# Sixteen extra short loads of K, issued once from SyncE in a single-core attention kernel

## The chip, the cores and the metric

The kernel runs on one core of a Trainium2 chip. The metric is the device time of one execution in microseconds (us), the median of several. A core has a matrix engine (TensorE, PE in the profile), VectorE (DVE), ScalarE (ACT), GpSimd (POOL) and SyncE (SP), each with its own instruction stream, and 16 DMA engines that move data between HBM and the on-chip memory. SyncE and ScalarE issue DMAs here; what SyncE issues goes to queue q1 of the profile, what ScalarE issues goes to q10.

## The reference

```python
B, H, Sq, Skv, Dh = 8, 16, 16, 2048, 256
def reference(q, k, v):
    scale = q.shape[-1] ** -0.5
    scores = jnp.einsum('bhqd,bhkd->bhqk', q, k) * scale
    attn = _softmax(scores, axis=-1)
    return jnp.einsum('bhqk,bhkd->bhqd', attn, v)
```

All tensors are bf16. K and V are 134 MB each, q and the output 1 MB each. Every element of K and V is used once, with only 16 queries per head.

## The kernel before

The 128 heads are worked off in 16 blocks of 8 heads (the loop index is g, r or j, `last` is 15). A block needs 16,384 rows of K and as many of V. The rows lie contiguously in HBM, so a load gives each of the 128 partitions one contiguous piece: K of a block comes in two DMAs of 4 MB (half blocks e = 0 and 1, 32 KB a partition, `load_k`, line 127), V of a block in one DMA of 8 MB (64 KB a partition, `load_v`, line 133). The last two blocks' V is cut into 3 and 9 pieces.

The on-chip tile SL has four slots of 4 MB: two hold V (VA, VB), two hold K (KA, KB). There is one buffer for each, so a load can only be issued when the matmuls that read the previous contents have ended. For a block, VectorE transposes K in place (line 196), PE forms Q·K (lines 309 and 310), VectorE takes the maximum, ScalarE the exponential, VectorE transposes the result, ScalarE and VectorE copy it into weights, and PE multiplies by V (line 332, 128 matmuls); ScalarE scales the result and stores it with a DMA on its own queue (line 301).

PE works Q·K of block r, then P·V of block r - 1. SyncE's stream follows this: after the first loads it runs a loop over j from 2 to 14 (line 143). A pass waits on c_qk (Q·K of half e of block j - 1 is done) and issues K of block j, for e = 0 and 1, then waits on c_pv (P·V of block j - 2 is done) and issues V of block j - 1. Nothing else stands in SyncE's stream there. After the loop come the last block's K in four pieces, the pieces of V for the last two blocks, and then a wait on c_ev (ScalarE has scaled the last result, line 155), the last store (line 156) and the wait for its landing (line 157).

A load tells that it is done through a semaphore: 16 are added for each DMA. The completion semaphores of K and V are s_k and s_v and their relatives; VectorE waits for K, PE for V.

Of the kernel before, what the change touches and what calls it, by code (L numbers as in the profile page):

```python
# [11 lines left out]
BF16 = mybir.dt.bfloat16  # L12
# [8 lines left out]
def bass_standalone__softmax_full_bidir__sampling_kernel(  # L21
# [16 lines left out]
    ku = k.rearrange("b h s d -> (b h s) d").rearrange("(u p t) d -> u p t d", p=128, t=T)  # L38
# [4 lines left out]
    with ExitStack() as es:  # L43
        ec = es.enter_context
# [9 lines left out]
        PTz = ec(nc.sbuf_tensor("PTz", [128, 2, T, 128], BF16))  # L54
        mk = ec(nc.sbuf_tensor("mk", [128, 1], F32))
        O_fin = ec(nc.sbuf_tensor("O_fin", [128, D], BF16))
        negm = ec(nc.sbuf_tensor("negm", [128, 1], F32))
        lsum = ec(nc.sbuf_tensor("lsum", [128, 2], F32))
        ltot = ec(nc.sbuf_tensor("ltot", [128, 1], F32))
# [6 lines left out]
        def sem(name):  # L66
            return ec(nc.semaphore(name))
# [6 lines left out]
        s_v0 = sem("s_v0")  # L74
        s_st = sem("s_st")
        s_fin = sem("s_fin")
        c_pool = sem("c_pool")
        c_qt = sem("c_qt")
        c_cq = sem("c_cq")
# [46 lines left out]
        def load_k(eng, g, e, slot, t0, n, s):  # L126
            eng.dma_start(SL[:, slot, t0:t0 + n, :], ku[2 * g + e, :, t0:t0 + n, :]).then_inc(s, 16)  # L127

        def on_sync(eng):
            def load_v(w, a, n):  # L130

                eng.wait_ge(c_pv, 8 * w + (a + n + C - 1) // C)
                eng.dma_start(VW[:, a:a + n, :], vb[w, :, a:a + n, :]).then_inc(s_p[w][a] if a else s_v, 16)  # L133

            eng.dma_start(QX, qh).then_inc(s_q, 16)  # L135
            for g, s0, s in ((0, VA, s_k0), (1, KA, s_k)):
                for e in range(2):
                    load_k(eng, g, e, s0 + e, 0, T, s[e])

            for e in range(2):  # L140
                eng.wait_ge(c_qk, 4 * e + 4)
                eng.dma_start(VW[:, T * e:T * e + T, :], vb[0, :, T * e:T * e + T, :]).then_inc(s_v0 if e else s_v, 16)
            with nc.Fori(2, last, engines=[SP]) as j:
                for e in range(2):
                    eng.wait_ge(c_qk, 8 * j + 4 * e - 4)
                    load_k(eng, j, e, KA + e, 0, T, s_k[e])
                load_v(j - 1, 0, 2 * T)
            for e in range(2):
                eng.wait_ge(c_qk, 8 * last + 4 * e - 4)
                load_k(eng, last, e, KA + e, 0, T // 2, s_k[e])  # L150
                load_k(eng, last, e, KA + e, T // 2, T // 2, s_kl[e])
            for w in PIECES:
                for a, n in PIECES[w]:
                    load_v(w, a, n)
            eng.wait_ge(c_ev, G + 1)
            eng.dma_start(oh[last], O_fin[:]).then_inc(s_fin, 16)
            eng.wait_ge(s_fin, 16)

# [146 lines left out]
        def on_tensor(eng):  # L305
# [48 lines left out]
            with nc.Fori(1, G + 1, engines=[PE]) as r:  # L354
# [20 lines left out]
                pv(lim)  # L375

        on_sync(nc.sync)
        on_gpsimd(nc.gpsimd)
        on_vector(nc.vector)
# [30 lines left out]
```

## Time and profile before

| | |
|---|---|
| median of 3 runs | 634.53 us (634.51 to 634.56) |
| the profiled execution's own time | 634.58 us |
| its span, first to last instruction | 633.3 us |
| PE, VectorE, ScalarE, GpSimd busy | 85%, 70%, 38%, 3% |
| moved | 270.56 MB, 427 GB/s over the span |
| granted TensorE clock | 0.976 |

How to read the lines shown below. A line of the DMA queues names a queue, its packets, its megabytes and the time its packets took as a share of 16 engines' span. The slices cut a stretch into 40 equal parts; a digit is the busy share in tenths. A line of the chain of waits, or of the timeline, begins with its start and its duration in us; "SPq" and "DVEq" are the instruction sequencers of SyncE and VectorE, and "DMA SL<-in_v_dram" is a load of V from its issue to its landing. A wait line names who waited for whom, the total in us, how often, and the longest. A line of DMA issues ends with the KB and the median us from issue to landing.

### The profile page before, as it was taken

The page shows a single profiled execution, that of the slowest core. Times are in us where ns is not written, and L with a number is a line of the kernel's source. Part 1 is how long each engine was busy: PE and PEld are TensorE (multiplying, and loading weights), DVE is VectorE, ACT ScalarE, POOL GpSimd, SP SyncE. Part 2 cuts the span into 40 slices and gives each one's busy share as a digit, 9 for nine tenths or more (in the row PEclk, how much of TensorE's full clock was granted, in tenths as well). Part 3 has the DMA queues.
Part 4 walks back from the last instruction along what each step waited for, and adds up shares of the span by engine and source line. Part 5 has one row for each costly group of instructions (what it writes and reads, how often), then busy time and mean ns, then how long its engine had stood idle before and what let it go on. Part 6 is the DMA issues. An engine that isn't in the chain of part 4 may idle for free.

```text
span 633.3 us, 8100 instructions
## 1 busy us (share of the span) xinstructions
PE 539.7 (85%) x3336; PEld 272.9 (43%) x2561; DVE 444.2 (70%) x285; ACT 241.8 (38%) x309; POOL 21.5 (3%) x18
## 2 busy tenths in 40 slices
PE   1659989889898897989979899797989979899998
PEld 0112824518244282542725336263362724518386
DVE  5989794765948658496575965759567595769750
ACT  1026542623326233352424425244252442623453
POOL 7600000000000000000000000000000000000000
PEclk9998989999898999989999899999998999999999
DMA  8999999999999999999999999999999999999997
GB/s 364 443 447 433 428 464 401 450 409 431 441 422 442 423 433 458 407 457 408 455 417 421 447 423 441 446 410 457 408 456 417 423 441 424 439 418 430 430 426 299
DMA packets 11234, 270.56 MB, mean 427 GB/s; under 512 B 1248, under 2 KB 3424, under 8 KB 3936
## 3 DMA queue, kind: packets, MB, share of 16 engines
q1 hardware_dynamic: 9072, 269.55, 98.8%
q10 hardware_dynamic: 2160, 0.98, 0.5%
q8 instruction: 1, 0.02, 0.0%
q14 instruction: 1, 0.01, 0.0%
HBM read 269.48 MB, written 1.05 MB: 427 GB/s over the span
## 4 chain that ended last, share of the span: by engine, by line
DMA 57%; PE 34%; DVE 5%; issue 3%; SPq 0%; DVEq 0%; ACT 0%
DMA SL<-in_v_dram 49%; PE O_ps L332 32%; DMA SL<-in_k_dram 8%; DVE SL L196 4%; PE S_ps L309 1%; PE S_ps L310 1%; DVE PTb L231 0%; DVE negm L220 0%; DVE PTa L229 0%; DVE PTz L203 0%; DVE PTz L205 0%; SPq L133 0%; SPq L127 0%; ACT O_fin L271 0%; SPq L135 0%
## 5 line engine op out<-in xcount | busy, mean ns | idle before, releaser
L196 DVE STREAM_TRANSPOSE SL<-SL 128x4096 f32<-128x4096 f32 x64 | 282.4, 4433 | 82.0 <-DMA SL<-in_k_dram 81.2
L309 PE MATMUL S_ps<-SL,QW 128*128 128x512 bf16 (+1 forms) x512 | 206.5, 403 | 68.9 <-DVE SL L196 59.1
L332 PEld LDWEIGHTS O_ps<-SL,PTz 128*128 128x128 bf16 x2048 | 198.6, 98 | 103.1 <-DMA SL<-in_v_dram 79.3
L332 PE MATMUL O_ps<-SL,PTz 128*128 128x256 bf16 x2048 | 227.2, 273 | 12.9 <-DMA SL<-in_v_dram 11.5
L310 PE MATMUL S_ps<-SL,QW 128*128 128x512 bf16 (+1 forms) x512 | 204.8, 400 | 0.0
L309 PEld LDWEIGHTS S_ps<-SL,QW 128*128 128x128 bf16 (+1 forms) x512 | 74.3, 145 | 245.1 <-issue 155.3
L263 ACT ACTIVATE QW<-QT 32x256 bf16 x64 | 26.9, 420 | 203.0 <-PE S_ps L310 201.8
L277 ACT ACTIVATE PTz<-PTa 16x1024 bf16<-16x1024 bf16 x32 | 33.8, 1056 | 111.8 <-PE O_ps L332 100.0
L220 DVE TENSOR_REDUCE negm<-S_ps 128x1 f32<-128x2048 f32 x16 | 36.6, 2289 | 55.1 <-PE S_ps L310 55.1
L310 PE MATMUL X_ps<-QT,QW 128*128 128x512 bf16 x260 | 58.2, 379 | 0.0
L277 ACT ACTIVATE PTz<-PTb 16x1024 bf16<-16x1024 bf16 x48 | 50.6, 1055 | 10.9 <-ACT O_fin L271 10.1
L229 DVE STREAM_TRANSPOSE PTa<-P_sb 128x1024 bf16<-128x1024 bf16 x32 | 39.2, 1224 | 21.9 <-ACT P_sb L292 21.9
L277 ACT ACTIVATE PTz<-PTa,mk 32x1024 bf16<-32x1024 bf16 x48 | 54.3, 1130 | 0.0
L231 DVE STREAM_TRANSPOSE PTb<-P_sb 128x1024 bf16<-128x1024 bf16 (+1 forms) x32 | 39.0, 1219 | 0.0
L292 ACT ACTIVATE P_sb<-S_ps,negm 128x1024 bf16<-128x1024 f32 x32 | 35.3, 1109 | 5.9 <-DVE negm L220 5.9
L277 ACT ACTIVATE PTz<-PTb,mk 32x1024 bf16<-32x1024 bf16 x32 | 36.2, 1132 | 0.0
L271 ACT ACTIVATE O_fin<-O_ps,rinv 128x256 bf16<-128x256 f32 x16 | 7.6, 473 | 51.6 <-PE O_ps L332 51.6
L203 DVE TENSOR_SCALAR PTz<-PTb,mk 32x1024 bf16<-32x1024 bf16 x32 | 15.2, 476 | 0.0
L205 DVE COPY PTz<-PTa 16x1024 bf16<-16x1024 bf16 x32 | 13.5, 422 | 1.6 <-PE O_ps L332 0.6
L170 POOL COPY QT<-PTz 32x1024 bf16<-32x1024 bf16 x12 | 14.3, 1192 | 3.0 <-DVE PTz L187 2.3
L205 DVE COPY PTz<-PTb 16x1024 bf16<-16x1024 bf16 x16 | 6.8, 424 | 3.4 <-PE O_ps L332 3.0
L309 PE MATMUL S_ps<-PTz 128*128 128x512 bf16 x1 | 0.6, 609 | 9.7 <-ACT QW L263 9.7
(21 smaller groups left out, 38.8 us busy)
## 6 DMA issues: line engine op xcount, KB each, us to landing
SL<-in_k_dram SPq DMA_DIRECT2D x30, 4096.0 KB, 24.3
SL<-in_v_dram SPq DMA_DIRECT2D x2, 4096.0 KB, 21.9
SL<-in_k_dram SPq DMA_DIRECT2D x4, 2048.0 KB, 21.1
SL<-in_v_dram SPq DMA_DIRECT2D x1, 3584.0 KB, 21.0
SL<-in_v_dram SPq DMA_DIRECT2D x1, 2560.0 KB, 23.6
SL<-in_v_dram SPq DMA_DIRECT2D x1, 2048.0 KB, 25.0
SL<-in_v_dram SPq DMA_DIRECT2D x1, 1920.0 KB, 11.3
SL<-in_v_dram SPq DMA_DIRECT2D x1, 1600.0 KB, 11.7
```

The source lines that it names most:

```text
L196: eng.transpose(x, x).then_inc(c_kt, 1)
L203: ins = eng.tensor_scalar(out=dst, in0=src, scalar1=m, scalar2=None, op0=ALU.mult)
L205: ins = eng.tensor_copy(dst, src)
L220: eng.tensor_reduce(out=negm[:], in_=S_ps[:].rearrange("p c n -> p (c n)"), axis=AX.X, op=ALU.max, negate=True).then_inc(c_mx, 1)
L229: eng.transpose(fa[:, 1024 * h:1024 * h + 1024], P_sb[:, 16 + 1024 * h:16 + 1024 * h + 1024]).then_inc(c_pt, 1)
L231: eng.transpose(fb[:, 1024 * h:1024 * h + n], P_sb[:, 1024 * h:1024 * h + n]).then_inc(c_pt, 1)
L263: eng.activation(dv, src(a), ACTF.Copy, scale=scale).then_inc(c_qw, 1)
L277: eng.activation(dst, src, ACTF.Copy, scale=m if x else 1.0).then_inc(c_cp, 1)
L292: eng.activation(P_sb[:, 16 + 1024 * h:16 + 1024 * h + 1024], sv, ACTF.Exp, bias=negm[:], scale=1.0, accum_out=lsum[:, h:h + 1]).then_inc( ...
L309: return eng.matmul(dst, w, x, start=start, stop=stop, skip_group_check=not check)
L310: return eng.add_instruction(mybir.InstMatmult(name=nc.get_next_instruction_name(), engine=PE, start_tensor_calc=start, stop_tensor_calc=stop,
L332: ins = eng.matmul(O_ps[:, 0:D], PTz[:, t // T, t % T, :], VW[:, t, :], start=(t == 0), stop=(t == 2 * T - 1))
```

## The change

In the pass j = 5 of SyncE's loop, behind the two loads of K and ahead of the wait for V, SyncE issues 16 more DMAs. The n-th one reads 64 + 8n elements from the start of each of the first n partitions' pieces of K (rows 32 KB apart in HBM) into n partitions of a new tile JK, each into columns of its own. They share a semaphore, s_jk, and SyncE waits for its 256 ahead of the last store. No other instruction reads JK. The comparison of j with 5 is made in every pass.

```diff
+        JK = ec(nc.sbuf_tensor("JK", [16, 2112], BF16))
...
+        s_jk = sem("s_jk")
...
                 for e in range(2):
                     eng.wait_ge(c_qk, 8 * j + 4 * e - 4)
                     load_k(eng, j, e, KA + e, 0, T, s_k[e])
+
+                jj = eng.to_reg(j)
+                with eng.If_eq(jj, 5):
+                    at = 0
+                    for n in range(1, 17):
+                        w = 64 + 8 * n
+                        eng.dma_start(JK[0:n, at:at + w], ku[0, 0:n, 0, 0:w]).then_inc(s_jk, 16)
+                        at += w
                 load_v(j - 1, 0, 2 * T)
...
             eng.wait_ge(c_ev, G + 1)
+            eng.wait_ge(s_jk, 256)
             eng.dma_start(oh[last], O_fin[:]).then_inc(s_fin, 16)
             eng.wait_ge(s_fin, 16)
```

## The prediction

> **What bounds the kernel now.** I read the page first: the slices, the DMA queues, the chain that ended last.
>
> ```profile
> span 633.3 us, 8100 instructions
> ...
> DMA  8999999999999999999999999999999999999997
> ...
> DMA packets 11234, 270.56 MB, mean 427 GB/s; under 512 B 1248, under 2 KB 3424, under 8 KB 3936
> ...
> q1 hardware_dynamic: 9072, 269.55, 98.8%
> q10 hardware_dynamic: 2160, 0.98, 0.5%
> q8 instruction: 1, 0.02, 0.0%
> ...
> DMA 57%; PE 34%; DVE 5%; issue 3%; SPq 0%; DVEq 0%; ACT 0%
> ```
>
> The sixteen DMA engines are busy 99.3% of the span (98.8 + 0.5). The kernel is bound by bytes; the 34% of PE in the chain is there only because the chain steps onto PE whenever PE's end released the next load. Next I read the chain in the stretch of block 5, then SyncE's issues and waits there.
>
> ```profile
> 182.12 14.16 PE O_ps L332 x128
> ...
> 196.45 24.54 DMA SL<-in_v_dram
> 220.99 0.05 issue
> 221.03 14.16 PE O_ps L332 x128
> ...
> 235.35 24.58 DMA SL<-in_v_dram
> ```
>
> ```profile
> 169.12 8.35 SPq L127 DMA_DIRECT2D SL<-in_k_dram  x2
> 196.45 0.33 SPq L133 DMA_DIRECT2D SL<-in_v_dram  x1
> ...
> SPq L133 <- PE O_ps L332: 18.7, 1, 18.7
> ```
>
> The loop's j = 2 is the pass with its K pair at 57.33; one pass takes about 38.9 us (235.35 - 196.45), and j = 5 is the pass with the pair at 169.12. SyncE issues K of block 5 (two DMAs, the second ending at 169.12 + 8.35 = 177.47), then waits 18.7 us until the P·V matmuls of block 3 end, and issues V of block 4 at 196.45. V takes 24.54 us to land. It is 8.39 MB (128 rows of 64 KB), which at the page's mean of 427 GB/s needs 19.6 us. So at its issue some 4.9 us of K was still queued ahead, and V began to move at about 201.4. The queue does not run dry: a late issue costs nothing until it is 4 to 5 us late, while any time that a DMA engine spends on something else is lost for good, if that engine is the one that finishes last.
>
> **The change part by part.**
>
> *Issuing.* SyncE gets 16 more DMA issues between 177.47 and its wait that ends near 196.3.
>
> ```profile
> 1.19 2.10 SPq L127 DMA_DIRECT2D SL<-in_k_dram  x4
> ...
> 603.84 12.23 SPq L133 DMA_DIRECT2D SL<-in_v_dram  x9
> ...
> 631.70 0.34 SPq L156 DMA_DIRECT2D out_dram<-O_fin  x1
> ```
>
> An issue alone takes 0.33 us, four back to back took 2.10, or 0.53 each. Sixteen take 5.3 to 8.4 us; I take 8.4, and SyncE is done at 185.9, 10 us before the end of its wait. The wait on c_pv hides it. Were that cover gone, 4.9 us of queued K would be the next. Behind these issues on SyncE stand only V of block 4 and everything after it, none due before 196.3; PE waits for that V. Cost: 0.
>
> *The branch.* All 13 passes read j and compare it. SyncE has no such branch in this trace; DVE has, at the kernel's line 241.
>
> ```profile
> 52.10 0.04 DVEq L240
> ...
> 52.33 0.06 DVEq L241
> 52.38 0.15 issue
> 52.53 0.05 DVEq L244
> ```
>
> From 52.10 to the next branch's body at 52.53 is 0.4 us, an upper bound for compare and jump. It falls in the same wait for P·V, which the page's passes all have (the whole line-133 wait is 18.7 us at block 5). Cost: 0.
>
> *The final wait.* Ahead of the last store stands one more wait (256 on s_jk), long fulfilled by then. Two waits in a row need one more instruction. At 196.3 SyncE steps through two such steps before its DMA:
>
> ```profile
> 196.30 0.04 SPq L133
> 196.35 0.04 issue
> 196.39 0.03 SPq L133
> ```
>
> So an extra step costs 0.04 to 0.09 us, on the path that sets the end (ScalarE's last result, then the store). I take 0.08; nothing hides it.
>
> *The transfers.* 136 rows of 2·(64 + 8n) bytes, n = 1 to 16: 144 to 384 B a row, 41,344 B in all. Each DMA also makes completion packets. The price of a short packet comes from the last store, which has the rings to itself, and from the kernel's last loads, which end in rows of 1.5 KB:
>
> ```profile
> DMA packets 144, 0.07 MB, mean 109 GB/s; under 512 B 16, under 2 KB 144, under 8 KB 144
> ...
> q1 hardware_dynamic: 144, 0.07, 36.4%
> ...
> DMA  9999998979898999999999977764422322110000
> GB/s 486 369 364 369 461 404 338 512 292 466 318 466 333 435 394 379 389 415 389 410 364 394 338 266 266 266 236 169 179 97 113 118 102 87 72 41 31 15 31 15
> DMA packets 467, 1.12 MB, mean 280 GB/s; under 512 B 60, under 2 KB 186, under 8 KB 467
> ```
>
> The first pair is the window from 632.4 to 633.0 us: 36.4% of 16 engines over 0.6 us is 3.49 us of packet time for 144 packets (128 of 512 B, 16 completions), 24 ns each. A large packet moves 27 B per ns (269.55 MB in 98.8% of 16·633.3 us). 65.5 KB at that rate is 2.43 us, so a packet as such costs (3.49 - 2.43)/144 = 7.4 ns. The page's q10 row gives the same: 0.5% is 51 us for 2160 packets, again 24 ns.
>
> How n rows are spread is not in this trace; its 128-row DMAs put 9 packets on each engine (9072 = 63 DMAs x 16 x 9), that is, 8 whole rows and a completion. If each of the n rows goes to another engine, from the first on, the first engine gets one row of all sixteen DMAs: 4,224 B, 0.16 us, and 32 packets at 7.4 ns, 0.24 us, together 0.39 us; the last engine gets one row, 0.03 us. Below this lies an even spread, 8.5 rows and 16 completions an engine, about 0.28 us; above it all 136 rows on one engine, 1.53 us + 152 x 7.4 ns = 2.7 us. I take 0.39 for the first engine, since that is how whole rows are spread in the 128-row DMAs. [...]
>
> Does it reach the end? The second group above is the window from 626 to 630 us in slices of 0.1 us. Up to 628.2 all engines run; then they drop out one after the other, and in the last slices 15 to 31 GB/s is one engine alone. So engines carry different lags, and the last lies over 1 us behind half of the others. What a load waits for is the last. If the first engine is the last, all 0.39 us count; if another is, its own smaller share. Bounds 0 to 0.39, and I take the middle, 0.2.
>
> Sum: 0 + 0 + 0.08 + 0.2 = 0.28 us on a profiled execution of 633.3 us span. Around the span lies little: the same execution's own time was 634.58, the median of the three runs 634.53. Forecast 634.53 + 0.28 = **634.81**.
>
> **Rivals.**
>
> *Short rows stall their engine (slower).* The place is the first engine at about 201.4, between K and V of block 5. There a row is read from HBM, a completion must follow it, and the next row comes from another DMA. If the engine cannot overlap these, each costs a latency rather than 20 ns.
>
> ```profile
> out_dram<-O_fin SPq DMA_DIRECT2D x1, 64.0 KB, 1.5
> ```
>
> This store landed 1.5 us after issue, of which 0.34 was issue and 9 packets x 24 ns, 0.2, were moving: 0.9 us of latency. Paid by 16 DMAs: 14.5 us, 649. Paid by a third (four or five in flight at once): about 5 us, 639.5. It decides from about 0.1 us a DMA, where 16 of them pass 0.2%. Against it: in the last loads, where a piece has 8 rows of 1.5 to 3.5 KB an engine and then a completion, the digits stay at 9 across the piece boundaries until engines run out of work. For it: none of those rows is under 512 B, and 1248 packets under 512 B are all completions (78 DMAs x 16). [...] Chance 0.20.
>
> *SyncE is held by the number of DMAs in flight (slower).* V(3), two K and 16 loads make 19.
>
> ```profile
> SL<-in_v_dram SPq DMA_DIRECT2D x1, 1920.0 KB, 11.3
> SL<-in_v_dram SPq DMA_DIRECT2D x1, 1600.0 KB, 11.7
> ```
>
> The most that the trace shows is 8: of the nine pieces issued from 603.84 to 616.07 only the first (603.84 + 11.3 = 615.1) had landed. In packets per engine those are up to 72, more than the 27 + 32 = 59 here; so only a limit on DMAs, between 8 and 19, would bite. With a limit of 8, the two K and six loads go, the other ten and V go out after K landed at 201.4, at 0.47 us each, and V starts after some 5 us and a latency of 0.9: 6 us of empty queue, 640.5. Chance 0.10.
>
> *All rows on one engine, the last one.* 2.7 + 0.08 us: 637.3. Chance 0.02; the spread of the 128-row DMAs speaks against it.
>
> *A code load.* SyncE's program grows; the one instruction load inside the span (q8, 0.02 MB) shows that such loads share the engines. At 27 B/ns 16 KB is 0.6 us, on one engine: at most 635.5, so no change of the verdict. Chance 0.04, held in "same".
>
> *Faster.* The short rows shift the engines against each other by up to 0.4 us; if they now collide less in HBM, the rate rises. Passes of 38.9 us move 16.8 MB, 431 GB/s, and q1's 27 B/ns x 16 is 432 GB/s, so hardly anything is there to gain. For 0.2% the remaining 430 us would have to run 0.3% faster: 633.2. Chance 0.05.
>
> *It does not do what it says.* j runs from 2 to 14 and is 5 once; if the branch were never taken the final wait on 256 could not end, so the loads run.
>
> **How the numbers follow.** Forecast 0.59 (634.5 to 635.2), code load 0.04, stalls 0.20, limit in flight 0.10, one engine 0.02, faster 0.05. Two tenths of a per cent are 1.27 us, about what a measurement of this kernel can tell from no change. Within it: 0.59 + 0.04 = 0.63, of which I give 0.01 up to each side for sizes misjudged: 0.61. Slower 0.20 + 0.10 + 0.02 + 0.01 = 0.33. Faster 0.05 + 0.01 = 0.06. The range 634.4 to 640.6 takes in the forecast and the code load (0.63), the limit (most of 0.10), one engine (0.02) and stalls up to 6 us, about half of 0.20; left out are heavier stalls and the faster case, under 0.2.
>
> **What would show it.** Right: the 136 rows in q1 as packets under 512 B, between K and V of block 5; SyncE's 16 issues done by 186; V of block 4 issued at 196.4 and landing 24.5 to 25.0 us later; passes after it still 38.9 us. Wrong: V(4) issued late (limit in flight); V(4) issued in time but landing over 26 us later (stall); later passes that differ from 38.9 us (the engines' phase).

## The result and the profile after

The changed kernel takes 635.68 us (median of 18 runs, 635.45 to 639.25) against 634.59 (18 runs, 634.42 to 634.81): the ratio is 1.0021, 95% interval 1.0015 to 1.0027. That is 1.09 us more, four times the 0.28 that were forecast, and it lies on the bound of 0.2%: the interval has points on either side of it. The profiled execution took 635.52 us, 0.94 more than the one of before.

The page of the changed kernel, queues and chain:

```profile
span 634.2 us, 8065 instructions
...
DMA packets 11506, 270.60 MB, mean 427 GB/s; under 512 B 1520, under 2 KB 3696, under 8 KB 4208
...
q1 hardware_dynamic: 9344, 269.60, 98.8%
q10 hardware_dynamic: 2160, 0.98, 0.5%
...
DMA 57%; PE 36%; DVE 4%; issue 2%; SPq 0%; ACT 0%; DVEq 0%
```

Queue q1 has 272 packets more, which is 136 rows and 136 completions (packets of 4 bytes, one from each engine behind its part of a load; the kernel before has 1248 of them for 78 DMAs, 16 each): each load of n rows uses n engines. The kernel is bound as before. The chain of waits around block 5, then SyncE's issues (start, duration, count), then its wait there:

```profile
196.38 25.65 DMA SL<-in_v_dram
222.03 0.05 issue
222.08 14.16 PE O_ps L344 x128
...
236.40 24.54 DMA SL<-in_v_dram
```

```profile
168.81 8.57 SPq L130 DMA_DIRECT2D SL<-in_k_dram  x2
177.52 5.69 SPq L156 DMA_DIRECT2D JK<-in_k_dram  x16
196.38 0.37 SPq L136 DMA_DIRECT2D SL<-in_v_dram  x1
...
SPq L136 <- PE O_ps L344: 12.9, 1, 12.9
```

SyncE is done with its 16 issues at 183.21 and still waits 12.9 us; V of block 4 is issued at 196.38, not later than before (196.45). But it lands 25.65 us after issue in place of 24.54, and that is the whole loss: 1.11 us, in one place. The next V takes 24.54 us again.

Where within that load? The trace has a record for every DMA packet, with start, duration and size. The engines work their packets back to back (98.8% of the span for q1, 0.5% for q10), so the row sizes tell them apart: the first to carry the 144 B row has 16 rows, the first to carry 160 B has 15, and so on. For twelve of the sixteen engines the records can be followed without doubt; times in ns:

```
rows on the engine                 16    15    14    13    11     9     8     7     6     5     4     3
rows and completions take         330   313   404   844   242   204   184   162   289   119    96    73
first packet of V over 2418      1791  1558  1337   890  1278  1000   413   362   204    50     0    30
```

A 64 KB packet of V takes 2418 ns; in the kernel before, the sixteen first packets of this load exceed that by 0.02 us in all (by 0.95 us in the trace of the run without the loads, below), here by 11.0 us. A row takes 14 to 25 ns and a completion 9 to 12, about as forecast, but the large packet behind them is late, on the whole the more the more loads the engine had. Five rows are the exception: the last four on the engine with 13 rows took 225, 180, 87 and 161 ns, the last on the engine with 14 rows 129 ns. (The engine with 6 rows also works short packets of queue q10 in between.) The engine that was last at the end of K has 6 rows and is through V's first packet at 203.91; the one with 13 rows began its rows 0.6 us earlier and is through at 204.54, so it has become the last. On it, the loss stands partly in its last rows and partly in the large packet.

### The profile page after: what moved, and what is told of

Its sections match the earlier page's. It is cut to its first block, busy times and chain, and to the rows that moved or that the text cites. A ratio compares the mean times of both kernels' runs of the same rounds, so it can differ in the third digit from the quotient of the medians.

```text
span 634.2 us, 8065 instructions
## 1 busy us (share of the span) xinstructions
PE 536.5 (85%) x3271; PEld 273.0 (43%) x2561; DVE 444.2 (70%) x285; ACT 241.7 (38%) x309; POOL 21.5 (3%) x18
## 3 DMA queue, kind: packets, MB, share of 16 engines
q1 hardware_dynamic: 9344, 269.60, 98.8%
## 4 chain that ended last, share of the span: by engine, by line
DMA 57%; PE 36%; DVE 4%; issue 2%; SPq 0%; ACT 0%; DVEq 0%
DMA SL<-in_v_dram 49%; PE O_ps L344 32%; DMA SL<-in_k_dram 8%; DVE SL L208 3%; PE S_ps L321 2%; PE S_ps L322 2%; DVE negm L232 0%; DVE PTz L215 0%; DVE PTz L217 0%; ACT P_sb L304 0%; SPq L136 0%; SPq L130 0%; ACT O_fin L283 0%; SPq L138 0%; DVEq L230 0%
## 5 line engine op out<-in xcount | busy, mean ns | idle before, releaser
L322 PE MATMUL X_ps<-QT,QW 128*128 128x512 bf16 x195 | 52.7, 379 | 3.4
```

The costliest lines, as they stand in the source:

```text
L322: return eng.add_instruction(mybir.InstMatmult(name=nc.get_next_instruction_name(), engine=PE, start_tensor_calc=start, stop_tensor_calc=stop,
```

## The experiments

Three theories were in play. **Theory 1**: every DMA costs an engine it runs on some 0.1 us beyond its packets, which a few large packets in flight hide for the first four or five. **Theory 2**: rows under 512 B cost it (the kernel before loads and stores none that short; its stores' rows have 512 B). **Theory 3**: the number of short packets in a row costs it, whatever DMA they belong to. All edits are to the loads in the changed kernel (and to JK's size and the count in the final wait); nothing computed is changed. Gains and losses are differences of medians to the kernel before on the same chip.

### Branch and wait without the loads

```diff
-                    at = 0
-                    for n in range(1, 17):
...
+                    eng.sem_inc(s_jk, 256)
```

> The comparison of j with 5 in every pass and the extra wait ahead of the last store stay, the 16 loads are left out (in their place SyncE adds 256 to s_jk). All theories: the branch is hidden by the wait for P.V, the extra wait costs 0.04 to 0.09 us; time 0.0 to 0.1 us above before, V of block 4 lands 24.5 us after its issue as in the kernel before. If more than 0.3 us of the 1.09 us remain here, the loss is not in the loads at all.

634.66 against 634.62 us, ratio 1.0001 (0.9992 to 1.0011). V of block 4 lands as before:

```profile
196.47 24.54 DMA SL<-in_v_dram
```

The loads make the loss. The extra wait costs nothing visible either: in the changed kernel ScalarE's last result ends at 632.61 (chain of waits, 632.14 + 0.47) and the store is issued at 632.64 (SyncE's timeline), the 0.03 us that it was before (631.67 and 631.70).

```profile
632.14 0.47 ACT O_fin L283
```

```profile
632.64 0.34 SPq L168 DMA_DIRECT2D out_dram<-O_fin  x1
```

### Longer rows

```diff
-                        w = 64 + 8 * n
-                        eng.dma_start(JK[0:n, at:at + w], ku[0, 0:n, 0, 0:w]).then_inc(s_jk, 16)
+                        p, at = (16, 256 * (n - 1)) if n < 9 else (0, 256 * (n - 9))
+                        eng.dma_start(JK[p:p + n, at:at + 256], ku[0, 0:n, 0, 0:256]).then_inc(s_jk, 16)
```

> The same 16 DMAs of 1 to 16 rows, but every row 512 B instead of 144 to 384 B. Theory 1 (each DMA's completion on an engine costs about 0.1 us that shows at the next large packet): the loss stays, 1.0 to 1.4 us, V of block 4 lands 25.6 to 25.9 us after issue. Theory 2 (rows under 512 B cost it): only the packets themselves remain, at most 16 x (27 + 9) ns = 0.5 us; V lands 24.6 to 25.0 us after issue.

636.10 us, 1.48 more, ratio 1.0031 (1.0017 to 1.0044).

```profile
196.35 25.74 DMA SL<-in_v_dram
222.09 0.05 issue
222.14 15.83 PE O_ps L342 x128
...
238.13 22.89 DMA SL<-in_v_dram
```

The loss stays with rows of 512 B (27 ns by the median): theory 2 falls. The 144 to 384 B rows took 20 ns by the median, less than those of 512 B. The P·V behind the late V was slower here (15.83 us), of which more below.

### Two DMAs of 128 rows, and four

```diff
-                    for n in range(1, 17):
-                        w = 64 + 8 * n
-                        eng.dma_start(JK[0:n, at:at + w], ku[0, 0:n, 0, 0:w]).then_inc(s_jk, 16)
+                    for n in range(2):
+                        w = 120
+                        eng.dma_start(JK[:, w * n:w * n + w], ku[0, :, 0, 0:w]).then_inc(s_jk, 16)
```

> Two DMAs of 128 rows of 240 B in place of the sixteen: 16 short rows on each of the 16 engines, but only 2 completions on each. Theory 1 (completions): only the packets, 16 x 15 ns + 2 x 6 ns = 0.25 us, time 0.3 us above before, V of block 4 lands 24.8 us after issue, its first packets take 2.42 us as usual. Theory 2 (short rows): every engine loses what the one with 16 rows lost in the change, 0.33 + 1.8 us, so time 2.1 us above before and V lands 26.6 us after issue.

The other run has `range(4)`:

> Four DMAs of 128 rows of 240 B: on each engine 32 short rows and 4 completions, 36 packets, against 32 packets where all 16 loads have 16 rows, and 18 with two such DMAs. Theory 1 (number of DMAs on an engine): only the packets count, 32 x 15 + 4 x 6 ns = 0.5 us; V of block 4 lands 25.0 us after issue, its first packets take 2.42 us each. Theory 3 (number of short packets ahead of a large one, 18 being still covered): loss as with 16 loads of 16 rows or more, 2.0 to 2.4 us, V lands 26.5 us or more after issue.

634.78 against 634.62 us, ratio 1.0002 (0.9992 to 1.0012), and 635.04 against 634.64, ratio 1.0006 (0.9996 to 1.0015); neither time is clear of noise. The landing of V, two DMAs first:

```profile
196.39 24.78 DMA SL<-in_v_dram
```

```profile
196.41 25.01 DMA SL<-in_v_dram
```

0.24 and 0.47 us more than 24.54: the packets and no more. 256 and 512 short rows cost less than the change's 136. With four DMAs no first packet of V is longer (the sixteen exceed 2418 ns by 0.00 us in all), behind 36 packets an engine; the change lost 1.8 us behind 32. Theory 3 falls. The two DMAs read the same 16 places in HBM, and 112 others at the same distances; whether reading these places again and again matters is settled by the run with a source on the chip, below.

### 16 rows in every load, and 8 or 32 such loads

```diff
-                        eng.dma_start(JK[0:n, at:at + w], ku[0, 0:n, 0, 0:w]).then_inc(s_jk, 16)
+                        eng.dma_start(JK[0:16, at:at + w], ku[0, 0:16, 0, 0:w]).then_inc(s_jk, 16)
```

> All 16 loads have 16 rows (256 in place of 136), so that each engine gets what the first one got in the change. Both theories: every engine loses about 0.33 + 1.8 us, so it no longer matters which is last: time 2.0 to 2.3 us above before, V of block 4 lands 26.5 to 26.8 us after issue. If instead only engines that fall out of step lose, the loss is under 1 us, since here all keep their distances.

For 8 and 32 loads the rows have 240 B:

> 8 loads of 16 rows of 240 B. Price per DMA beyond the first four or five: 0.16 + 3.5 x 0.14 = 0.65 us, V of block 4 lands 25.2 us after issue. One latency exposed once: 0.16 + 1.7 = 1.8 us, V lands 26.4 us after issue.

> 32 loads of 16 rows of 240 B, twice those of all_rings, on all engines. Theory 1 with a price per DMA beyond the first four or five (0.14 us each): 0.66 us of packets + 27 x 0.14 = 3.9 us, together 4.5 us, V of block 4 lands 29 us after issue. If it is one latency that is exposed once, however many loads there are: 0.66 + 1.7 = 2.4 us, V lands 26.9 us after issue.

8, 16 and 32 loads: 635.46, 636.64 and 640.58 us, that is 0.82, 2.02 and 5.94 more; ratios 1.0013 (1.0003 to 1.0022), 1.0034 (1.0022 to 1.0047) and 1.0098 (1.0081 to 1.0115). V of block 4 in this order:

```profile
196.49 25.28 DMA SL<-in_v_dram
```

```profile
196.50 26.52 DMA SL<-in_v_dram
```

```profile
196.26 29.74 DMA SL<-in_v_dram
```

Over 24.54 these are 0.74, 1.98 and 5.20 us. About 0.021 us a load is packets (0.33 us for 16), so 0.57, 1.65 and 4.5 are left: 0.135 us for each load between 8 and 16, 0.18 between 16 and 32; drawn back to zero, the line begins at four loads, which fits the four DMAs above (no run has five to seven). No single exposed latency does that, and since all engines have the same loads here, it is not a matter of engines that fall out of step. That the price rises with the count was not expected.

With 32 loads SyncE was held once, at the last of them: the two issues take 2.19 us in place of 0.9.

```profile
191.22 2.19 SPq L156 DMA_DIRECT2D JK<-in_k_dram  x2
```

### One engine alone

```diff
-                    for n in range(1, 17):
-                        w = 64 + 8 * n
-                        eng.dma_start(JK[0:n, at:at + w], ku[0, 0:n, 0, 0:w]).then_inc(s_jk, 16)
+                    for n, w in enumerate((73, 79, 83, 89, 97, 101, 103, 107, 109, 113, 127, 131, 137, 139, 149, 151)):
+                        eng.dma_start(JK[0:1, 152 * n:152 * n + w], ku[0, 0:1, 0, 0:w]).then_inc(s_jk, 16)
```

> 16 loads of one row each, of a prime number of elements (73 to 151), so that a load can use one engine alone: no other engine has anything to do. Theory 1, with a load waiting for its last engine: that engine loses 0.3 + 1.8 us as the first one did in the change; it reached its rows 1.6 us ahead of the last there, so the time rises by about 0.5 us and V of block 4 lands 25.0 us after issue; the fifteen others keep 2.42 us for their first packet of V. If the loss is shared by all engines (HBM), V's first packets are longer on several.

634.98 against 634.64 us, ratio 1.0007 (0.9997 to 1.0016): the time alone is not clear of noise, the trace shows more.

```profile
q1 hardware_dynamic: 9104, 269.56, 98.9%
```

```profile
196.42 24.89 DMA SL<-in_v_dram
```

The 32 packets over 9072 are 16 rows and 16 completions, so each load ran on one engine. The change's load of one row, of 72 elements, was a single packet (of 144 B), too: that the number of elements has to be a prime is not shown. By the packet records one first packet of V is 1.83 us longer, a second 0.40 (of the 1664 packets of 64 KB in the kernel before, three are 0.41 to 0.44 us longer), the others not. The engine lost 0.3 + 1.83 = 2.1 us, and V lands 0.35 later: the rest was the lead that this engine had on the last.

### One load in each pass

```diff
-                with eng.If_eq(jj, 5):
...
+                for m in range(2, last):
+                    with eng.If_eq(jj, m):
+                        at = 120 * (m - 2)
+                        eng.dma_start(JK[0:16, at:at + 120], ku[0, 0:16, 0, 0:120]).then_inc(s_jk, 16)
```

> 13 loads of 16 rows of 240 B, one in each pass of the loop in place of all in one pass. If the price comes from loads that follow each other without anything long between them: only packets, 13 x 0.024 = 0.3 us, time 0.2 to 0.5 us above before, V's first packets no longer than in the kernel before. If each load costs an engine 0.16 us wherever it stands: 13 x 0.16 = 2.1 us.

634.83 against 634.69 us, ratio 1.0003 (0.9993 to 1.0013); V lands 24.57 us after issue in block 5's pass, and its first packets exceed 2418 ns by 0.85 us in all, about what they do without any load (0.95).

```profile
196.49 24.57 DMA SL<-in_v_dram
```

Apart from each other 13 such loads cost 0.14 us, within the noise, where 8 in a row cost 0.82: the price is for loads that follow each other.

### More to move in each load

```diff
-                        eng.dma_start(JK[0:n, at:at + w], ku[0, 0:n, 0, 0:w]).then_inc(s_jk, 16)
+                        p, at = 16 * (n % 8), 1024 * (n // 8)
+                        eng.dma_start(JK[p:p + 16, at:at + 1024],
+                                      ku[0, 0:16, 0:4, :].rearrange("p t d -> p (t d)")).then_inc(s_jk, 16)
```

> All 16 loads have 16 rows, as in all_rings, but rows of 2 KB: on each engine 32 KB, 16 x (0.083 + 0.006) = 1.4 us of packets in place of 0.33. If a load's end has to be waited for while the next few run (a rate of one load per 0.16 to 0.2 us and engine, whatever it moves up to that time), the moving hides in it: together still about 2 to 2.4 us, V of block 4 lands 26.5 to 26.9 us after issue. If the price is added to the moving: 1.4 + 1.65 = 3.1 us, V lands 27.6 us after issue.

638.16 against 634.69 us, 3.47 more, ratio 1.0055 (1.0037 to 1.0073).

```profile
196.41 28.20 DMA SL<-in_v_dram
224.60 0.05 issue
224.65 16.98 PE O_ps L343 x128
```

3.66 us later than 24.54: more than 1.4 us of packets and 1.65 us of price together. The moving does not hide the price. Here the rows themselves are recorded longer: 141 ns by the median, where the first ones take 84. In its companion, 16 loads of 128 rows of 240 B, SyncE was held and V issued late, so that its sum isn't clean:

> 16 loads of 128 rows of 240 B: on each engine 128 short rows and 16 completions, 16 x (8 x 15 + 6) = 2.0 us of packets. If the price of 0.10 to 0.16 us a load is added to what the load moves: 2.0 + 1.65 = 3.7 us, V of block 4 lands 28.2 us after issue. If eight rows are enough to hide it: 2.0 to 2.3 us, V lands 26.6 to 26.9 us after issue.

638.40 against 634.60 us, ratio 1.0055 (1.0039 to 1.0072). SyncE's timeline, then the chain of waits:

```profile
177.62 24.25 SPq L155 DMA_DIRECT2D JK<-in_k_dram  x16
202.16 0.34 SPq L136 DMA_DIRECT2D SL<-in_v_dram  x1
```

```profile
202.16 21.88 DMA SL<-in_v_dram
```

V landed at 224.04, 3.05 us after the kernel before (220.99), between "hidden" (2.0 to 2.3) and "added" (3.7). The 16 issues took 24.25 us; the eighth alone took 15.13 by its record. By count (an estimate from 9 packets a load and engine, behind V's rest and two K), some 80 packets an engine were then waiting. So SyncE can be held; what the hold counts is not shown. The 59 packets an engine of the change did not bring it on.

### A source on the chip

```diff
-                        eng.dma_start(JK[0:n, at:at + w], ku[0, 0:n, 0, 0:w]).then_inc(s_jk, 16)
+                        eng.dma_start(JK[0:16, w * n:w * n + w], QT[0:16, 0:w]).then_inc(s_jk, 16)
```

with w = 120 throughout.

> The 16 loads of all_rings with a source on the chip: rows of 240 B of the tile QT, which is only read at that time, in place of rows of K. If the price is the reading from HBM: packets alone, 0.4 us, V of block 4 lands 24.9 us after issue. If it is the change from one DMA to the next, or its completion: as all_rings, 1.9 to 2.1 us, V lands 26.4 to 26.6 us after issue.

637.97 against 634.60 us, 3.37 more, ratio 1.0060 (1.0037 to 1.0084).

```profile
196.28 26.73 DMA SL<-in_v_dram
223.01 0.05 issue
223.06 15.83 PE O_ps L342 x128
...
239.05 24.55 DMA SL<-in_v_dram
```

V takes 2.19 us longer to land, about as with rows from HBM (1.98): the price isn't the reading from HBM. The profiled execution took 638.42 us, 3.8 more; the rest of that comes behind this V. P·V took 15.83 us in place of 14.16, and V of block 5 is issued at 239.05, 3.7 us later than before (235.35), and lands as much later. That slower P·V alone does this is not shown: with 512 B rows it took as long, and V of block 5 landed only 1.1 us late.

## Why the prediction was right and wrong

**The outcome.** The time lies in the stated range (635.68 in 634.4 to 640.6), but the likeliest call, no change by 0.2%, is neither borne out nor refuted by 0.21%. Lying in the range does not bear out the sum: the range had been drawn wide for the rivals, and the loss stayed at 1.09 us because the engines with the most loads had a lead on the last one, which the prediction knew of in general but not engine by engine. With 16 rows in every load, on all engines, the loss was 2.02 us, 0.34%. That the time did not leave the call far behind was partly luck.

**Issuing and the branch at 0.** Right. 5.69 us of issues against a bound of 8.4, and 12.9 us of wait left over. Without the loads the time rose by 0.04 us, which is noise.

**The final wait at 0.08.** Too much: from ScalarE's last result to the store it is 0.03 us with the wait and without it. The second wait is one more instruction, as forecast (17 ns on SyncE, line 167 of the changed kernel), but it stands at 617.1 us, ahead of the wait for ScalarE and not behind it.

**The transfers' packets.** Right. First engine: 0.33 us by the records against 0.39. The choice of n engines for n rows, which the prediction took from the 128-row DMAs, is confirmed by the 272 additional packets and by the run on one engine.

**The step that failed** is the sum's "0.39 for the first engine ... Bounds 0 to 0.39, and I take the middle, 0.2": it priced a load by its packets alone, and put the passage from load to load at nothing in the sum. A load in a row of loads costs each of its engines 0.135 to 0.18 us more from about the fifth on. On the engines of the change that is up to 1.8 us, and 1.1 of it passes the lags and reaches the end. The rows from which the price was made could not show it: the last store is one DMA of 144 packets, and q10's DMAs stand apart.

**The stall rival**, given 0.20, had the place (between K and V of block 5) and the kind of loss. Its price was too high: it took 0.9 us a DMA, or a third of that, where 0.135 to 0.18 was measured, and its sign, V landing over 26 us after issue, did not come (25.65, between that and the 25.0 of the forecast). Of its grounds, rows under 512 B and the read from HBM fall. That a completion follows each row and the next row comes from another DMA is what is left. The time shows mostly in the large packet behind the rows, and in part in the last rows.

**SyncE held by the number of DMAs**, 0.10: not in the change. With 32 loads, 31 went out behind two K without a hold, so a limit on DMAs between 8 and 19 is excluded; the hold that was seen came sooner with 128-row loads (at the eighth) than with 16-row loads (at the 32nd).

**Lags of the engines.** Right that only the last counts: 2.1 us lost on one engine came out as 0.35. Wrong that the last stays the last: in the change another overtook it. The queued K was a little overrated, too: by the packet records of the kernel before, V's first packets begin at 199.23 to 201.08, not at about 201.4, so the earliest engine would have run dry 2.8 us after V's issue and not 4.9. Nothing hung on it, since V was issued in time.

**Faster, a code load.** Neither: the passes after block 5 are as before, and the page's instruction queues show the same two packets (q8 and q14; the prediction spoke of one).

What the price consists of stays open. Number and length of rows, HBM as source, and the branch are excluded as causes. Nor is it a crowd of engines writing to the same 16 partitions of JK: one engine alone lost as much (1.83 us in the packet behind its rows), and in the run with 2 KB rows successive loads went to different partitions. What is left belongs to a DMA as such, its completion or the passage to the next DMA. No run parts these two; all loads of a run report to one semaphore, and no run gives them separate ones. The rise from 0.135 to 0.18 us is unexplained.

## What to carry to other kernels

Where the DMA engines bound the kernel, count DMAs in a row as well as bytes: past the first four, a load with one short row an engine cost each engine that it used about 0.15 us, though its packets took 0.02. Put many short rows into one DMA (256 rows in two cost 0.16 us of time, 256 in sixteen 2.02), or spread the DMAs between long transfers (13, one a pass, 0.14); neither the 0.16 nor the 0.14 is clear of noise. A load waits for its last engine, so the same work costs little on an engine with a lead (2.1 us lost on one engine, 0.35 at the landing).

## What the runs showed beyond this

The price hardly stands where it arises: most short packets of the change are recorded at 14 to 25 ns each, and the next large packet is up to 1.8 us too long. In longer bursts it reaches the short packets as well: with 16 rows in every load single rows took up to 368 ns, and with 32 loads single completions up to 365 ns.

Behind a late V, P·V was at times slower, and PE's granted clock lower. In the change and in the run with 16 rows in every load, PE waited 2.0 and 2.8 us for V of block 4, the clock was 1.00 from 221 to 243 us, and P·V took 14.16 us. With 512 B rows and with the source on the chip the wait was 2.05 and 3.0 us, the clock 0.92 and P·V 15.83 us. With 128 rows, 2 KB rows and 32 loads the wait was 3.9, 4.5 and 6.0 us, the clock 0.84 each time and P·V 16.8 to 17.0 us. The window from 221 to 243 us of the run with 2 KB rows, then of the kernel before (the column ahead of the DMA share is PE's clock):

```profile
221.00:243.00 22.00, 18.35 (x136) 14.35 (x133) 11.99 (x11) 4.67 (x5) 0.00 (x0) 0.84 0.98 414
```

```profile
221.00:243.00 22.00, 19.48 (x151) 14.17 (x140) 15.56 (x14) 10.95 (x11) 0.00 (x0) 1.00 1.01 435
```

That the longer wait lowers the clock is an inference; 2.05 us came with 0.92, and 2.8 us with 1.00.

Slower P·V puts off the issue of the next V, but K is still queued ahead of it, so it need not cost anything. With 512 B rows the next V was issued 2.8 us late and landed 1.1 us late, no later than V of block 4 had been. With 2 KB rows 0.3 us were added in this way, with the source on the chip 1.65. Why these differ is not shown.
